# Attention and MLP on one core: Strassen's scheme in the second product of one more pair, and new orders

## The chip, the cores and the metric

The kernel runs on one core of a Trainium2 chip. Five engines work side by side, each through its own queue of instructions: TensorE (PE, with its weight loads shown apart as PEld), VectorE (DVE), ScalarE (ACT), GpSimd (POOL) and SyncE (SP, which issues the DMAs). The metric is device time of one execution in microseconds. The kernel before takes 564.89 us (median of 3 runs, 564.1 to 565.23).

## The reference

Four sequences of 768 tokens, eight heads of 64. Each query sees its neighbours at a distance under 16 and, in place of all the rest, one summary for every block of 32 keys:

```python
k_sum = k.reshape(B, H, nb, block, D).max(axis=3)        # block = 32, nb = 24
v_sum = v.reshape(B, H, nb, block, D).mean(axis=3)
scores_l = scale * np.matmul(q, k.transpose(0, 1, 3, 2)) # kept where |i - j| < 16, else -1e9
scores_s = scale * np.einsum('bhsd,bhnd->bhsn', q, k_sum) + np.log(block)
a = softmax(np.concatenate([scores_l_m, scores_s], axis=-1))
x = np.matmul(a, np.concatenate([v, v_sum], axis=2))     # -> 3072 tokens x 512
h = x @ w_in                                             # 512 x 2048
g = 0.5 * h * (1.0 + erf(h / sqrt(2)))
out = g @ w_out                                          # 2048 x 512
```

All results are fp32. The two weight matrices come as 64-bit floats.

## The kernel before, in words

The 3072 tokens are twelve chunks of 256. A chunk's attention is two units (four heads each), so there are 24 units; a chunk's MLP is a first product (x by `w_in`, `phase1`) and a second (g by `w_out`, `phase2`). For fp32 accuracy each operand is split into a high and a low f16 part, and each product is three f16 matmuls: high by high, high by low, low by high. ACT makes most high parts (steps that end in `_hi`), DVE all low parts (`_lo`), and POOL some casts of k, q, p and x.

A unit: `scores` (PE, into the PSUM tile `ps_s`), `add_mask`, `maximum`, `exponent` (ACT, eight groups of 128), `recip`, then the normalized p is split into `p_h` and `p_l` and turned by two DMA transposes (`turn`), and `values` (PE, into `ps_v`) makes x. The first six units are of another kind: their scores are fp32 matmuls, with the mask added by PE (`f_mask`), and in units 0 to 3 (`TURNED`) p is not split but turned by fp32 matmuls (`p_turn`, `p_keep`), and the values are fp32 as well. For p there are two ways to split: `split_hi` and `split_lo` in eight groups that also normalize, or `p_norm` for the whole tile and then a cast and one `p_lo`.

Chunks 2p and 2p+1 are pair p. For pairs 2 to 5 the first product uses Strassen's scheme: seven products (`product p j m`) for each quarter j of the hidden columns, instead of eight, with sums of x (`sx_add`) and of `w_in` (`t_add`); `keep` copies partial sums out of PSUM, `h_add` adds them. For the last pair, 5, the second product uses the scheme too: sums of g (`s_add`, `s_hi`, `s_lo`), sums of `w_out` (`u_add`, `u_hi`, `u_lo`), and seven products `s_product m j` of 12 matmuls, each 256 columns wide; `phase2` matmuls are 512 wide. PSUM has `ps_s`, `ps_v` and a ring of five banks, handed out in the order in which they come free.

While no data is there yet, PE runs `warm` matmuls on a tile of ones, called fillers here: 54 of them before.

What sets the order on every engine is a list written out by hand (`ORDER`): 1585 steps, each the name of a function and its numbers. The program calls them in that order, every engine takes its instructions in the order of the list, and waits are set by what each instruction reads and writes. Loads and stores go through SP's queue in the list's order too.

Of the kernel before, what the change touches and what calls it, by code (L numbers as in the profile page):

```python
# [88 lines left out]
maximum_p 4, exponent_p 4, recip 3, wi_lo 4 0, p_norm 3, wo_bits 4 0, wi_lo 6 1, p_turn 3 1, f_mask 5,
phase1h 0 2 1, take_hi 2, p_keep 3 1, wi_hi 3 0, p_turn 3 0, wo_bits 4 1, wi_lo 3 1, wi_lo 3 0, wo_bits 4 2,  # L90
recip 4, take_lo 2, wi_bits 0 1, wo_hi 4, p_keep 3 0, gelu 0 1, fetch_w_out 0, load_v 3, fetch_w_in 5, load_v 4,
scores 5, load_vs 3, wo_lo 4, phase1h 0 6 1, values 3, phase1h 0 3 0, phase1h 0 3 1, take_hi 3, wi_bits 0 2,
wo_bits 0 0, take_lo 3, g_hi 0 1, gelu 0 7, wo_bits 0 1, wi_bits 5 0, wi_lo 4 1, wi_hi 0 1, wi_lo 0 1, wo_bits 0 2,
# [15 lines left out]
phase2 0 3, phase2 0 7, phase2 0 6, k_sums 1 0, g_hi 1 2, scores 6, values 5, s_k_hi 8, take_hi 5, store 0 0,
add_mask 6, prep_k_end 1 1, g_lo 1 6, g_lo 1 2, maximum 6, exponent 6, s_q_hi 8, store 0 1, s_k_hi 7, take_lo 5,  # L110
prep_v 1 0, q_lo 7, load_q 9, fetch_v 2 0, k_lo 8, k_sums 1 1, recip 6, prep_v 1 1, q_lo 8, load_vs 6, phase2 1 5,
k_lo 7, phase2 1 3, phase1 2 7, phase2 1 2, phase1 2 2, scores 7, phase1 2 3, g_hi 1 7, split_hi 6, split_lo 6,
g_lo 1 7, add_mask 7, phase2 1 7, scores 8, load_q 10, load_k 9, turn 6 0, q_hi 9, v_hi 6, gelu 2 7, g_hi 2 7,
s_k_hi 9, gelu 2 2, gelu 2 3, v_lo 6, q_lo 9, turn 6 1, phase1 2 4, phase1 2 6, values 6, maximum 7, k_lo 9,
add_mask 8, maximum 8, prep_v 2 0, g_lo 2 7, exponent 7, recip 7, p_norm 7, p_hi 7, load_v 7, load_q 11, put 0 0,
put 0 1, fetch_kx 3 0, exponent 8, recip 8, prep_kx 3 0, load_vs 7, fetch_k 2 0, load_k 10, scores 9, k_hi 10,
take_hi 6, v_hi 7, g_hi 2 2, phase1 2 0, store 1 1, gelu 2 6, s_q_hi 10, g_hi 2 3, g_hi 2 6, gelu 2 0, p_lo 7,
t_add 3 0, take_lo 6, turn 7 0, phase2 1 6, phase1 2 5, v_lo 7, prep_k 2 0, k_lo 10, turn 7 1, load_v 8, values 7,
phase1 2 1, t_add 2 1, split_hi 8, split_lo 8, g_hi 2 0, take_hi 7, take_lo 7, g_lo 2 6, t_add 0 1, gelu 2 5,
g_hi 2 5, g_lo 2 5, add_mask 9, load_k 12, load_k 11, k_hi 11, fetch_k 2 1, gelu 2 4, store 1 0, load_vs 8, put 1 0,  # L120
gelu 2 1, g_lo 2 0, v_hi 8, phase1 3 4, phase1 3 1, q_lo 10, g_lo 2 3, prep_k_end 2 0, maximum 9, fetch_v 3 0,
load_q 12, v_lo 8, k_lo 11, load_v 9, turn 8 0, scores 10, g_lo 2 2, g_hi 2 1, g_lo 2 1, t_add 0 2, add_mask 10,
load_k 13, prep_k 2 1, maximum 10, gelu 3 1, exponent 9, recip 9, phase1 3 3, gelu 3 4, gelu 3 3, g_hi 3 4,
g_hi 3 3, g_lo 3 4, p_norm 9, g_hi 3 1, q_hi 12, k_hi 12, k_lo 12, turn 8 1, fetch_kx 3 1, load_k 14, load_vs 9,
fetch_v 3 1, phase1 3 7, phase1 3 0, phase1 3 6, g_hi 2 4, gelu 3 0, g_hi 3 0, prep_v 3 0, g_lo 3 1, exponent 10,
g_lo 2 4, t_add 0 3, q_hi 11, q_lo 11, g_lo 3 0, phase2 2 0, values 8, phase1 3 2, phase1 3 5, gelu 3 2, k_sums 2 0,
p_hi 9, recip 10, scores 11, p_lo 9, q_lo 12, p_norm 10, turn 9 0, turn 9 1, add_mask 11, prep_kx 3 1, v_hi 9,
gelu 3 6, gelu 3 5, gelu 3 7, g_hi 3 6, g_hi 3 5, s_p_hi 10, x_take 8, sx_hi 2 0, g_lo 3 5, maximum 11, v_lo 9,
# [1147 lines left out]
```

## Time and profile before

| | |
|---|---|
| median of 3 runs | 564.89 us |
| profiled execution | 564.51 us |
| its span, first to last instruction | 562.7 us |
| PE busy | 556.1 us (99%), 6126 matmuls |
| DVE busy | 454.2 us (81%) |
| ACT busy | 379.5 us (67%) |
| POOL busy | 42.2 us (8%) |

The span is the profiled execution without what lies around it, 1.8 us. A busy time is the time in which at least one instruction of the engine was under way. The ends of matmuls are modelled, so how fast PE really goes is read from the steps between starts. In the profile's lists "idle before" is how long the engine had nothing under way before a group's instructions, and what ended that. The columns "out<-in" are the program's tiles; several functions share a line where a helper records them.

### The profile page before, as it was taken

How to read it: one execution, taken by the hardware profiler on the slowest of the kernel's cores; microseconds unless marked ns; L12 is line 12 of the kernel's file. 1: busy time of each engine (PE TensorE's matmuls, PEld its weight loads, DVE VectorE, ACT ScalarE, POOL GpSimd, SP SyncE). 2: the span in 40 equal slices, each digit the busy share in tenths (PEclk: the TensorE clock that was granted, in tenths of full speed). 3: DMA queues.
4: the chain of work that ended last, by engine and by line, in shares of the span. 5: the costliest groups of instructions: out<-in, count | busy, mean ns of one | idle time of the engine just before them, and what ended most of it. 6: DMA issues, size and time to landing. Idle time of an engine off the chain costs nothing.

```text
span 562.7 us, 14579 instructions
## 1 busy us (share of the span) xinstructions
PE 556.1 (99%) x6126; PEld 392.5 (70%) x6126; DVE 454.2 (81%) x699; ACT 379.5 (67%) x940; POOL 42.2 (8%) x50
## 2 busy tenths in 40 slices
PE   9999999999999999999999999999999999999997
PEld 4788886457888555587665767756578756668886
DVE  4999999989999888989989386969745685797750
ACT  2995976548979858879596589795577545346530
POOL 0010000000121001001213000111000010000000
PEclk9999999999999999999999999999999999999999
DMA  8894686677887765434543534512314100001002
GB/s 330 327 406 162 214 245 176 200 226 209 223 255 172 162 163 129 131 64 128 142 131 90 157 80 101 133 32 64 71 54 130 25 2 1 19 1 57 1 1 76
DMA packets 70994, 74.40 MB, mean 132 GB/s; under 512 B 44816, under 2 KB 49808, under 8 KB 70928
## 3 DMA queue, kind: packets, MB, share of 16 engines
q1 hardware_dynamic: 70928, 73.46, 45.9%
q8 instruction: 48, 0.79, 0.6%
q14 instruction: 18, 0.15, 0.1%
HBM read 54.90 MB, written 6.29 MB: 109 GB/s over the span
## 4 chain that ended last, share of the span: by engine, by line
PE 89%; ACT 4%; DMA 3%; DVE 3%; SPq 1%; issue 1%; POOL 0%; ACTq 0%; DVEq 0%; POOLq 0%
PE bank L969 25%; PE bank L1024 10%; PE bank L1026 10%; PE bank L1025 10%; PE bank L1129 5%; PE bank L928 4%; PE bank L941 4%; PE bank L930 4%; PE bank L929 4%; PE ps_v L875 3%; PE bank L917 2%; PE ps_v L1129 2%; PE ps_s L760 2%; PE ps_s L742 2%; ACT s L788 1%; DMA v<-in_vw_dram 1%
## 5 line engine op out<-in xcount | busy, mean ns | idle before, releaser
L1024 PE MATMUL bank<-w_out_h,gh 128*128 128x512 f16 x320 | 121.4, 379 | 0.0
L1025 PE MATMUL bank<-w_out_l,gh 128*128 128x512 f16 x320 | 121.3, 379 | 0.0
L1026 PE MATMUL bank<-w_out_h,gl 128*128 128x512 f16 x320 | 121.3, 379 | 0.0
L1011 DVE SCALAR_TENSOR_TENSOR gl<-g,gh 128x512 f16<-128x512 f32 x92 | 62.1, 693 | 17.8 <-ACT gh L1007 17.7
L969 PEld LDWEIGHTS <-w 128*128 128x128 f16 x640 | 62.0, 98 | 10.5 <-issue 1.5
L969 PEld LDWEIGHTS <-w_in 128*128 128x128 f16 x576 | 55.5, 98 | 11.3 <-issue 0.8
L788 ACT ACTIVATE s<-s,s_top 128x128 f32<-128x128 f32 x144 | 55.6, 389 | 7.7 <-DVE s_top L779 7.6
L1026 PEld LDWEIGHTS <-gl 128*128 128x128 f16 x320 | 31.3, 98 | 37.8
L981 DVE TENSOR_TENSOR g<-bank,late 128x512 f32<-128x512 f32 x48 | 32.9, 685 | 27.9 <-PE bank L969 19.4
L1007 ACT ACTIVATE gh<-g 128x512 f16<-128x512 f32 x92 | 54.8, 623 | 0.5
L1024 PEld LDWEIGHTS <-gh 128*128 128x128 f16 x320 | 31.3, 98 | 33.1
L1025 PEld LDWEIGHTS <-gh 128*128 128x128 f16 x320 | 31.3, 98 | 32.6
L975 ACT ACTIVATE late<-bank 128x512 f32<-128x512 f32 x48 | 28.3, 591 | 32.4 <-PE bank L969 27.5
L969 PE MATMUL bank<-x,w_in 128*128 128x256 f16 x384 | 47.1, 273 | 0.0
L1000 ACT ACTIVATE g<-g 128x512 f32<-128x512 f32 x48 | 29.6, 623 | 21.9 <-DVE g L981 21.9
L969 PE MATMUL bank<-stage,w 128*128 128x256 f16 x320 | 44.1, 273 | 0.0
L969 PE MATMUL bank<-x,w 128*128 128x256 f16 x320 | 43.8, 273 | 0.0
L928 PE MATMUL bank<-x,w_in 128*128 128x256 f16 x144 | 39.3, 273 | 0.0
L929 PE MATMUL bank<-x,w_in 128*128 128x256 f16 x144 | 39.3, 273 | 0.0
L930 PE MATMUL bank<-x,w_in 128*128 128x256 f16 x144 | 39.3, 273 | 0.0
L1000 ACT ACTIVATE g<-bank 128x512 f32<-128x512 f32 x48 | 28.0, 590 | 13.3 <-PE bank L930 7.3
L850 DVE SCALAR_TENSOR_TENSOR v_hl<-v,v_hl 128x1024 f16<-128x1024 f32 x20 | 25.0, 1248 | 6.0 <-ACT v_hl L847 6.0
(206 smaller groups left out, 1146.0 us busy)
## 6 DMA issues: line engine op xcount, KB each, us to landing
v<-in_vw_dram SPq DMA_DIRECT2D x22, 512.0 KB
stage<-in_w_out_dram SPq DMA_DIRECT2D x8, 1024.0 KB
q<-in_qd_dram SPq DMA_DIRECT2D x24, 256.0 KB
out_dram<-ot SPq DMA_DIRECT2D x23, 256.0 KB
k<-in_kd_dram SPq DMA_DIRECT2D x18, 320.0 KB
stage<-in_vb_dram SPq DMA_DIRECT2D x6, 768.0 KB
stage<-in_kp_dram SPq DMA_DIRECT2D x4, 768.0 KB
gh<-in_w_in_dram SPq DMA_DIRECT2D x2, 1024.0 KB
```

The source lines that it names most:

```text
L788: nc.scalar.activation(self.s32[:, gs], score[:, gs], AF.Exp, bias=self.top[:, g : g + 1], scale=QKSCALE, accum_out=self.den[:, g : g + 1],)
L928: nc.tensor.matmul(dst, wh, xh, start=(k == 0), stop=False)
L929: nc.tensor.matmul(dst, wh, xl, start=False, stop=False)
L930: nc.tensor.matmul(dst, wl, xh, start=False, stop=(k == NCC - 1))
L969: nc.tensor.matmul(dst, l, r[:, k], start=(first and e == 0 and k == 0 and n == 0), stop=(k == KH - 1 and n == 2), skip_group_check=True,)
L1000: nc.scalar.activation(g, h, AF.Gelu, scale=1.0 / (SC_X * SC_WI))
L1007: nc.scalar.activation(gh, g_slot(c, i), AF.Copy, scale=SC_G)
L1011: nc.vector.scalar_tensor_tensor(out=gl, in0=g_slot(c, i), scalar=SC_G, in1=gh, op0=ALU.mult, op1=ALU.subtract)
L1024: nc.tensor.matmul(t, gh[:, f, js], w_out_h[:, f, :], start=(n == 0), stop=False)
L1025: nc.tensor.matmul(t, gh[:, f, js], w_out_l[:, f, :], start=False, stop=False)
L1026: nc.tensor.matmul(t, gl[:, f, js], w_out_h[:, f, :], start=False, stop=(n == NFC - 1))
L1129: nc.tensor.matmul(acc[:, t * NH : (t + 1) * NH], a[:, f, js], b[:, f], start=(first and j == 0 and t == 0 and f == 0 and n == 0), stop=(f ...
```

## The change

The order of nearly all steps is new, and with it several functions:

- Pair 4's second product goes by Strassen's scheme as pair 5's does. `s_add`, `s_hi`, `s_lo`, `s_product`, `s_keep`, `s_sum`, `s_end` get the pair as their first number. The sums of `w_out` are made once, earlier, and used by both pairs; they and the sums of g move to other tiles (`homes`, `left`), for which small tiles are joined (`misc`, `kk`). Sixteen `phase2` steps go (80 to 64), 24 `s_product` and two `s_last` come.
- No p is split in eight groups any more: all 21 units that split p use a whole cast on ACT (`s_p_hi`) and a whole `p_lo`. p is normalized by ACT in eight groups for 13 units (`s_norm`, 2 before) and by DVE for 11.
- POOL casts nothing: k, q, p and x are cast on ACT. (POOL also makes no copies of the means of v.)
- The factor 1/8 on the scores moves into `add_mask`, so `maximum` and `exponent` of masked tiles need none; units 0 to 5 keep it.
- Unit 1's scores go to two banks of the ring in place of `ps_s` (`BANKED`). Three units are turned by PE in place of four (`TURNED`). 25 fillers instead of 54. The exponential's table is asked for in `setup`.

```diff
 PAIRS = (2, 3, 4, 5)
+BANKED = (1,)
 WIDE = 6
-TURNED = 4
+TURNED = 3
...
-load_q 0, fetch_k 0 0, load_eye, load_m16, fetch_w_in 2, fetch_k 0 1, fetch_wh 7 1, load_q 1, load_ind,
+fetch_k 0 0, load_m16, load_q 0, fetch_k 0 1, fetch_wh 1 1, load_q 1, fetch_w_in 4, warm 2 9, warm 3 3, f_mask 0,
...
     def setup():
         nc.gpsimd.memset(ones, 1.0)
+        nc.scalar.activation(stats[1][2][:, :1], ones[:, :1], AF.Exp)
...
+        def ps(self, e):
+            if self.banked:
+                return bank.use(f"sc{self.nm}{e}", 4)
+            return ps_s[:, e * QCOLS : (e + 1) * QCOLS]
...
-                out=self.s32.rearrange("p (h j) -> p h j", **shape), in0=m, scalar=SC_WI,
-                in1=ps_s.rearrange("p (h j) -> p h j", **shape), op0=ALU.mult, op1=ALU.add,
+                out=self.s32.rearrange("p (h j) -> p h j", **shape), in0=ps_s.rearrange("p (h j) -> p h j", **shape), scalar=QKSCALE,
+                in1=m, op0=ALU.mult, op1=ALU.add,
...
+            if raw:
+                nc.vector.tensor_scalar_mul(self.top, self.top, QKSCALE)
...
+    SP2 = LAST - 1
 
     def g_slot(c, i):
-        if c // 2 == LAST:
+        if c // 2 >= SP2:
             n = ((9, 7), (5, 8))[c % 2][i // 4]
...
     def g_part(c, i):
-        return (a[:, 2 * i : 2 * i + 2, :].rearrange("p f j -> p (f j)") for a in g_hl[c % 2])
+        if c // 2 == LAST:
+            w = {(0, 0): (0, 0), (0, 1): (1, 1), (1, 1): (1, 0)}[c % 2, i // 4]
+            cs = slice(i % 4 * CH, (i % 4 + 1) * CH)
+            return (a[w][:, :, cs] for a in (w_in_h, w_in_l))
+        return (a[:, 2 * i : 2 * i + 2, :] for a in g_hl[c % 2])
...
+    left = parts_of(flat16)
+    U1, U2, U4, U3 = range(4)
+    homes = {
+        U1: parts_of([misc, late[:, 3072:]]),
+        U2: parts_of([kk, k32[:, 1024:].bitcast(F16)]),
+        U4: left[24:],
+        U3: [a[:, 2 * q : 2 * q + 2, NH:] for q in range(4) for a in (w_out_h, w_out_l)],
+    }
...
+    def s_acc(p, a):
+        if a == SZ:
+            return ps_v if p == LAST else ps_s[:, :QCOLS]
+        return bank.use(f"s{p}{a}", {SX: 19, SY: 5}[a])
...
+    s_sums = {SP2: [a[:, :512] for a in dens], LAST: hsum}
...
-    def s_product(m, j):
-        acc = S_PROD[m][0]()
+    def s_product(p, m, j):
+        acc = s_acc(p, S_PROD[m][0])
         for t in range(CH // P):
-            s_tile(m, j, t, acc)
+            s_tile(p, m, j, t, acc)
```

How the order moves, at three places. On PE at the program's start, from unit 0's scores to its first turn (L742 and L775 are `scores`, L917 and L965 fillers, L828 and L876 `p_turn`, L571 and L596 the sums of v). Before:

```order
L742 MATMUL ps_s<-w_out_l,q_0_83 64x32 x4
L917 LDWEIGHTS ones
L917 MATMUL bank_66<-ones 64x512
...
L742 MATMUL ps_s<-w_out_l,q_1_84 64x32 x4
...
L917 MATMUL bank_63<-ones 64x512
L828 MATMUL bank_64<-mask_sb,s_0_90 128x128 x4
L571 MATMUL bank_65<-w_out_h 88x256 x6
```

and after:

```order
L775 MATMUL ps_s<-w_out_l,q_0_83 64x32 x4
L965 LDWEIGHTS ones
L965 MATMUL bank_65<-ones 64x512
...
L775 MATMUL bank_67<-w_out_l,q_1_84 64x32 x2
...
L965 MATMUL bank_63<-ones 64x512
...
L775 MATMUL ps_s<-misc,q_0_83 64x24 x4
L775 MATMUL ps_s<-w_out_l,q_0_83 64x32 x4
L876 MATMUL bank_64<-misc,s_0_90 128x128 x4
L876 MATMUL bank_65<-misc,s_0_90 128x128 x4
L596 MATMUL bank_63<-w_out_h 88x256 x6
```

Unit 1's scores go to the banks 66 and 67, and the scores of unit 2 (q_0 again) now stand ahead of unit 0's first turn. After unit 0's scores came 30 fillers and now come 12; after unit 1's came 6 and now comes 1.

On ACT at the same place (L788 and L833 are `exponent`, L394 and L416 `wi_hi`, L822 and L870 `s_norm`, L831 and L879 `p_keep`). Before:

```order
L788 ACT_TABLE_LOAD
L788 ACTIVATE s_0_90,s_den_96<-ps_s,s_top_95 128x128 x8
L394 ACTIVATE w_in_71<-w_2_77 128x2x256
L822 ACTIVATE s_0_90<-s_0_90,s_rec_97 128x128 x8
...
L788 ACTIVATE s_1_91,s_den_99<-ps_s,s_top_98 128x128 x8
L394 ACTIVATE late<-w_2_77 128x2x256
L831 ACTIVATE pt<-bank_64 128x512
```

and after:

```order
L382 ACT_TABLE_LOAD
L382 ACTIVATE s_rec_100<-ones 128x1
L833 ACTIVATE s_0_90,s_den_96<-ps_s,s_top_95 128x128 x8
L416 ACTIVATE w_in_72<-w_1_76 128x2x256
L870 ACTIVATE s_0_90<-s_0_90,s_rec_97 128x128 x8
L833 ACTIVATE s_1_91,s_den_99<-bank_66,s_top_98 128x128 x4
L833 ACTIVATE s_1_91,s_den_99<-bank_67,s_top_98 128x128 x4
L416 ACTIVATE w_in_73<-w_0_75 128x2x256
L833 ACTIVATE s_0_90,s_den_96<-ps_s,s_top_95 128x128 x8
L416 ACTIVATE late<-w_0_75 128x2x256
L879 ACTIVATE pt<-bank_65 128x512
```

The table is loaded first, unit 1's exponentials read two banks, and unit 2's come before unit 0's turned p is copied.

On PE in pair 4 (L969 and L1017 are `product`, L1024 to L1026 `phase2`, L1194 `s_product`; gh and gl are the parts of g). Before:

```order
L969 MATMUL bank_66<-stage,w_in_73 128x256
L1024 LDWEIGHTS gh_106
L1024 MATMUL bank_64<-w_out_h,gh_106 128x512
...
L1025 MATMUL bank_66<-w_out_l,gh_106 128x512
L1026 LDWEIGHTS gl_107
L1026 MATMUL bank_66<-w_out_h,gl_107 128x512
```

and after:

```order
L1017 MATMUL bank_65<-stage,w_in_73 128x256
L1194 LDWEIGHTS gh_106
L1194 MATMUL bank_67<-w_out_h,gh_106 128x256
L1194 LDWEIGHTS gh_106
L1194 MATMUL bank_67<-w_out_l,gh_106 128x256
L1194 LDWEIGHTS gl_107
L1194 MATMUL bank_67<-w_out_h,gl_107 128x256
```

Where matmuls of 512 columns stood among pair 5's first products, matmuls of half that width stand now, and the bank they write stays theirs through the pair.

## Rows read from the trace of the kernel before

**Rows 1.** The page's table of engines: busy us, share of the span, instructions.

```profile
PE 556.1 (99%) x6126; PEld 392.5 (70%) x6126; DVE 454.2 (81%) x699; ACT 379.5 (67%) x940; POOL 42.2 (8%) x50
```

**Rows 2.** The page's chain that ended last, shares of the span by engine.

```profile
PE 89%; ACT 4%; DMA 3%; DVE 3%; SPq 1%; issue 1%; POOL 0%; ACTq 0%; DVEq 0%; POOLq 0%
```

**Rows 3.** Stages: length, then busy us (instructions) by engine, clock, DMA share.

```profile
10.00:35.00 25.00, 25.00 (x442) 18.01 (x440) 24.09 (x41) 21.93 (x78) 0.78 (x1) 1.00 0.95 361
60.00:100.00 40.00, 40.00 (x361) 31.20 (x360) 39.62 (x54) 31.13 (x60) 0.00 (x0) 1.00 0.67 196
...
150.00:200.00 50.00, 50.00 (x614) 35.80 (x612) 47.38 (x70) 40.90 (x101) 7.24 (x7) 1.00 0.85 198
200.00:250.00 50.00, 48.01 (x559) 30.57 (x557) 45.74 (x74) 38.95 (x115) 3.09 (x3) 1.00 0.44 112
250.00:300.00 50.00, 50.00 (x600) 34.47 (x598) 45.01 (x64) 42.37 (x95) 10.16 (x9) 1.00 0.50 133
300.00:350.00 50.00, 50.00 (x521) 34.70 (x520) 34.52 (x61) 35.60 (x90) 4.31 (x4) 1.00 0.45 113
...
500.00:562.70 62.70, 59.24 (x512) 49.89 (x510) 35.63 (x56) 25.82 (x48) 0.00 (x0) 0.99 0.09 30
```

Engines there stand in the order PE, PEld, DVE, ACT, POOL.

**Rows 4.** PE in order of time, 126 to 132: start, duration, instruction.

```profile
125.83 0.27 PE L928 MATMUL bank<-x,w_in 128*128 128x256 f16 x1
...
127.80 0.38 PE L1024 MATMUL bank<-w_out_h,gh 128*128 128x512 f16 x1
...
130.39 0.27 PE L928 MATMUL bank<-x,w_in 128*128 128x256 f16 x1
```

**Rows 5.** The chain in order of time: start, length, piece and its instructions.

```profile
9.46 6.16 PE bank L917 x28
...
529.11 5.24 PE bank L1129 x48
...
556.62 2.63 PE bank L1129 x24
```

**Rows 6.** Groups on PE: count | busy us, mean ns | idle before.

```profile
L875 PE MATMUL ps_v<-pt,v_hl 128*64 128x64 f16 x960 | 19.1, 197 | 0.0
...
L1129 PEld LDWEIGHTS <-gh 128*128 128x128 f16 x128 | 12.5, 98 | 1.4
...
L828 PE MATMUL bank<-mask_sb,s 128*128 128x128 f32 x64 | 8.5, 278 | 0.0
...
L875 PE MATMUL ps_v<-pt,v_hl 128*64 128x64 f32 x64 | 2.6, 226 | 0.2 <-issue 0.2
```

**Rows 7.** Groups on DVE and ACT, in the same columns.

```profile
L1011 DVE SCALAR_TENSOR_TENSOR gl<-g,gh 128x512 f16<-128x512 f32 x92 | 62.1, 693 | 17.8 <-ACT gh L1007 17.7
...
L805 ACT ACTIVATE p_h<-s,s_rec 128x128 f16<-128x128 f32 x88 | 26.8, 390 | 0.0
...
L810 DVE SCALAR_TENSOR_TENSOR p_l<-s,s_rec,p_h 128x128 f16<-128x128 f32 x88 | 24.4, 348 | 0.0
...
L840 DVE TENSOR_TENSOR p_l<-s,p_h 128x1024 f16<-128x1024 f32 x9 | 10.9, 1216 | 1.2 <-POOL p_h L834 1.2
...
L718 ACT ACTIVATE qh<-q 128x512 f16<-128x512 f32 x11 | 6.8, 619 | 5.0 <-DMA q<-in_qd_dram 5.0
...
L822 ACT ACTIVATE s<-s,s_rec 128x128 f32<-128x128 f32 x16 | 4.9, 392 | 0.1
...
L837 ACT ACTIVATE p_h<-s 128x1024 f16<-128x1024 f32 x2 | 2.1, 1047 | 0.0
```

**Rows 8.** In order of time, from the start and from 57 on.

```profile
5.92 1.75 DVE L530 TENSOR_REDUCE ks<-w_out_l 128x48 f32<-128x1536 f32 x1 [5.92 <-DMA w_out_l<-in_kp_first_dram]
...
9.53 1.22 DVE L776 TENSOR_REDUCE s_top<-ps_s 128x8 f32<-128x1024 f32 x1 [1.85 <-PE ps_s L742]
...
11.04 1.28 ACT L788 ACT_TABLE_LOAD   x1 [11.04 <-DVE s_top L779]
...
59.93 0.27 PE L928 MATMUL bank<-x,w_in 128*128 128x256 f16 x1
```

More of the change, by code (lines that the diff above doesn't have):

```diff
@@ L89 @@
[L89 to L93, printed above, removed]
@@ L109 @@
[L109 to L113, printed above, removed]
@@ L114 @@
[L114 to L128, printed above, removed]
@@ new lines @@
+s_k_hi 15, keep 2 0 2, store 3 1, load_vs 13, put 3 1, exponent 14, h_add 2 0 3, product 2 0 4, product 2 0 3,
+gelu 5 0, g_hi 5 0, s_k_hi 16, v_hi 13, t_lo 1 1, k_lo 15, q_lo 16, values 12, recip 14, p_lo 13, q_lo 15,
+prep_kx 3 4, phase2 3 6, product 2 1 5, product 2 2 1, scores 15, h_add 2 0 1, v_lo 13, g_lo 5 0, k_lo 16, gelu 4 0,
+g_hi 4 0, g_lo 4 0, add_mask 15, store 3 0, keep 2 1 1, gelu 4 4, keep 2 2 0, gelu 5 4, t_hi 2 1, g_hi 4 4,
+product 2 1 7, keep 2 1 2, t_hi 2 0, x_take 12, product 2 3 1, scores 16, product 2 1 4, turn 13 1, turn 13 0,
@@ new lines @@
+g_lo 7 0, load_v 19, load_vs 19, gelu 6 5, gelu 7 5, v_hi 19, keep 3 2 1, v_lo 19, keep 3 3 0, store 5 1, x_take 18,
+product 3 2 7, product 3 2 5, g_hi 7 5, g_hi 7 1, turn 19 0, load_v 20, turn 19 1, put 5 0, load_q 23, keep 3 2 2,
+g_lo 7 5, h_add 3 2 3, add_mask 21, k_lo 22, put 5 1, load_vs 20, s_norm 20, g_hi 6 5, s_q_hi 22, sx_hi 4 1,
+product 3 3 6, product 3 2 3, product 3 2 4, values 19, h_add 3 2 1, q_lo 22, scores 22, g_lo 7 1, sx_hi 4 0,
+keep 3 3 1, product 3 3 7, gelu 6 6, gelu 6 2, g_hi 6 6, gelu 7 6, phase2 6 0, g_lo 6 5, sx_lo 4 0, u_add 0 0,
@@ new lines @@
+phase2 6 3, scores 23, phase2 6 2, v_hi 21, sx_hi 4 5, g_hi 6 7, keep 4 0 0, sx_hi 4 4, sx_lo 4 4, u_add 0 3,
+v_lo 21, s_norm 21, s_p_hi 21, gelu 7 3, g_lo 6 7, p_lo 21, u_add 0 4, maximum 22, sx_lo 4 5, add_mask 23,
+sx_add 4 6, product 4 0 6, keep 4 0 1, exponent 22, product 4 0 2, phase2 6 7, phase2 6 6, values 20, u_hi 0 0,
+store 6 0, g_hi 7 3, load_v 22, load_vs 22, v_hi 22, store 6 1, g_hi 7 6, h_add 4 0 0, recip 22, sx_lo 4 3,
+p_norm 22, maximum 23, sx_hi 4 6, sx_lo 4 6, g_lo 7 3, x_take 20, v_lo 22, product 4 1 1, product 4 0 7, turn 21 0,
@@ L793, in exponent_p @@
         def exponent_p(self):
-            self.exponent(ps_s)
+            if not self.banked:
+                return self.exponent(ps_s)
+            for e in range(2):
+                self.exponent(self.ps(e), e)
         def recip(self):
```

469 lines of the change are left out of this document (255 added, 214 removed).

## Prediction

> **What bounds the kernel now.** I read the page's table of engines first, then the chain of waits, then the busy time by stage, and last the groups of instructions by line. TensorE (PE) is busy for 556.1 us of a span of 562.7 [rows 1], and the chain that ends last is 89% PE [rows 2]. A busy PE is not a full PE, so I looked at steps from start to start: eighteen 256-column matmuls take from 125.83 to 127.80, 109.4 ns each, and twelve 512-column ones from 127.80 to 130.39, 215.8 ns each [rows 4]. Per column that is 0.427 and 0.421 ns, at a granted clock of 1.00 [rows 3], the 2.4 GHz level. There is no slack inside a busy PE there, so what shortens its work shortens the kernel as long as the others keep up. PE's idle time is 2.0 us in 200:250 and 3.5 us behind its last matmul [rows 3]; the last piece begins at 556.62 [rows 5], and behind it stand only a copy and a store.
>
> The others do not keep up everywhere. VectorE (DVE) is busy for 24.1 of 25 us in 10:35, 39.6 of 40 in 60:100 and 47.4 of 50 in 150:200 [rows 3]. In the first 100 us it is a second bound, and PE fills its gaps there with 54 fillers. ScalarE (ACT) is densest in 250:300, 42.4 of 50, where GpSimd (POOL) works 10.2 us beside it.
>
> **The change part by part.** The sum is made against the profiled execution, 564.5 us: a span of 562.7 and 1.8 around it.
>
> Second product of the last-but-one pair. 192 matmuls of 512 columns go (16 `phase2` steps of 12) and 336 of 256 columns come. By the step above 192 x 0.2158 = 41.4 us go; for the half-wide ones the last pair's own rows count, 48 in 5.24 us [rows 5], so 336 x 0.1092 = 36.7 us come. Term: -4.7 us, all of it on PE's path, where nothing hides it. Its price on the others, 16 additions and 12 more low parts at 0.69 us on DVE and 12 more high parts at 0.62 on ACT [rows 7], lies after 400, where both have room (ACT 25.8 of 62.7 us from 500 on, [rows 3]). The narrow place there is the ring of five banks, of which the pair's sums hold two while the next pair begins.
>
> A rule speaks against this edit. By rows, 256 and 512 columns cost the same per column [rows 4], and the weight load of a half-wide matmul, 98 ns [rows 6], still fits under its 109 ns. The Trainium skill (TensorE: Matmul & The Clock Gate, section Back-to-back issue gap) gives a sustained spacing of about 81 ns at 128 columns and 131 at 512, set by load and matmul together, which would make wide matmuls far cheaper per column. By an estimate from that page, with 98 ns at 256 columns, this term would be 32.9 - 25.2 = +7.7 us. The trace disagrees at 512 columns, 215.8 ns against 131, and the measurement decides.
>
> Unit 3. PE no longer turns its p in fp32; it is split, and turned by DMA, like the later units'. PE loses a quarter of the turns of four units (8.5 us) and a quarter of their fp32 values (2.6 us in the row shown; I take the same for the other half, which is as many), and gets 48 of the small f16 matmuls, 48/960 of 19.1 us [rows 6]: -2.1 - 1.3 + 1.0 = -2.4 us of PE work. DVE gets a whole low part of p (1.22, [rows 7]) and one of v, and `values 3` gets a new wait, for two DMA transposes that stand in SyncE's queue behind loads of 0.25 to 1 MB. Behind it on PE wait a `phase1h`, the scores of unit 5 and all of chunk 1.
>
> Fillers and the new start. 29 of 54 fillers go; 28 took 6.16 us [rows 5], so 6.4 us of PE. But a filler stands where PE would wait, so this and unit 3's 2.4 are worth only what the start itself gains. The place to read it is the first `phase1` of chunk 1, at 59.93 [rows 8]: from there on PE has the same work before and after, but for the second product. That step follows `take_lo 3` on DVE, and DVE after 9.53 [rows 8] hardly waits. The DVE instructions up to and including it sum to 53.3 us before (64 steps) and 50.7 after (61), by the mean durations of their groups. That is 2.6 us sooner. DVE's first work waits until 5.92 for K [rows 8], which stands behind a 256 KB load of q and now goes first; with that and a shorter gap before 9.53 I take 0.7 more. The table load at 11.04, 1.28 us [rows 8], moves into set-up, and unit 1's scores get banks of their own instead of waiting for unit 0's exponentials to leave `ps_s`; both relieve ACT and PE, and give nothing while DVE is the later one. Term for unit 3 and the start together: -3.3 us. Bounds: -8.8 (6.4 + 2.4) if PE never misses the fillers, and +2.5 (a loss) if DVE's two new parts for unit 3 push everything behind them. I take -3.3, since DVE's 99% in 60:100 leaves no more.
>
> Whole p splits, no casts on POOL, the scale of scores. For eleven units eight-part splits go. On ACT, eight rows of 0.39 become eight equal ones that normalize (L805 and L822, [rows 7]), and 19 whole copies of 1.05 come on top: +20 us. The 31 casts of k, q and x from POOL cost ACT 0.62 to 0.72 each: +20. With the pair's high parts (+7.5) and four copies of v and its means (+4), ACT gets +51 us: 379.5 becomes 431, 78% of the new span. DVE loses 24.4 us of L810, gets 12 whole low parts (14.6) and the pair's 28 rows (19.3), and drops 18 multiplications of 0.17, since the scale moves into the mask's addition: about +10, to 464 us, 84%. While both stay ahead of PE this costs nothing on its path. The cover is thin in one place: between `product 3 1 4` and `phase2 6 4` the new order holds 37.6 us of ACT by these rows against 26.9 of PE, so ACT must enter that stretch ahead. Bounds: -2.0, if the waits in 200:250 go and none come, and +21, if ACT is never ahead (third rival). I take 0: the row nearest is today's, 2.0 us of waits inside, and I let as much come as goes.
>
> Sum: -4.7 - 3.3 + 0 = -8.0, so 556.5 for a profiled execution. The median of the runs, 564.89, lies 0.4 above the profiled one; I predict 557.0.
>
> **The rivals.**
> All of it comes back, because DVE does not set the start. Then -4.7 - 8.8 - 2.0 = -15.5: 549 to 552. For it: PE is at 40.0 of 40 in 60:100, beside DVE's 39.6, so it need not be waiting for DVE there. Against it: DVE at 99%. Chance 0.18.
>
> The start gives nothing and banks run short. Pair 5's products have three banks in place of five; if in each of four rounds PE waits for a `keep` and an `h_add` (0.6 + 0.7 us, estimated from the 0.62 and 0.69 in [rows 7]), 5.2 us stand against 4.7: 563 to 566. For it: three reuses in the new order with only 0.9 to 1.3 us of PE work between a bank's last write and its next use. Against it: the order before has one such reuse of 1.3 us in pair 2, and PE idles only 2.0 us in that whole stretch. Chance 0.08.
>
> ACT becomes the bound, and the kernel slower. The places are chunk 2's `phase1` (33.7 us of ACT in the new order against 23.4 of PE) and the end of pair 3 (37.6 against 26.9). If ACT cannot work ahead there, because its exponentials wait for scores that PE makes just before, PE waits 10.3 + 10.7 = 21 us: 564.5 - 8.0 + 21 = 577.5; half of it is 567. It decides from 8 us of such waits on. For it: ACT's 42.4 of 50 in 250:300 before POOL's 10.2 come over. Against it: 35.6 of 50 in the next stretch [rows 3] leaves room on both sides. Chance 0.12.
>
> Half-wide matmuls cost more than half. If their 98 ns of weight load lay bare, 336 x 98 ns = 32.9 us come on top: 589. The last pair's 336 of this shape show nothing of it [rows 5]. The skill's rule would show in this way. Chance 0.01.
>
> That the change does not do what it says is out: the new order has 768 matmuls of 512 columns in place of 960, and 25 fillers.
>
> **How the numbers follow.** The forecast, with 553 to 561 as its own range, has 0.61. What a measurement of this kernel can tell from no change is about 0.2%, 1.1 us. Faster: 0.61 + 0.18 + half of the bank rival, 0.04, and 0.02 for a mild ACT rival, 0.85. Within 0.2%: the other half, 0.04. Slower: 0.10 + 0.01 = 0.11. The range for 8 in 10 reaches into the first rival below and through most of the second above: 550.5 to 563.5.
>
> **What would show it.** Right: 256 matmuls in each of the three 512-column lines and 672 half-wide ones at 109 ns; the first `phase1` of chunk 1 at 56 to 57; PE idle for under 4 us between there and its last matmul; DVE above 97% in 10:60. The start's term is wrong if chunk 1 begins at 59 or later, or before 55. The third part is wrong if waits of PE for ACT's `keep`, `gelu` or `store` sum to over 4 us. The prediction as a whole falls if PE idles more than 8 us after 60.

## The result, and the profile after

The changed kernel takes 556.77 us (median of 4 runs, 556.61 to 557.98) beside 564.5 for the kernel before on the same chip: ratio 0.987, 95% interval 0.9847 to 0.9892. Predicted were 557.0. The profiled execution took 556.6 with a span of 554.8, 7.9 us less than before. The total came out as forecast, but two of the three terms behind it did not: their errors cancel.

The page's table of engines and the chain that ended last, for [rows 1, 2]:

```profile
PE 544.9 (98%) x6241; PEld 402.8 (73%) x6241; DVE 453.2 (82%) x638; ACT 425.3 (77%) x1005; POOL 0.8 (0%) x9
...
PE 94%; DMA 3%; DVE 1%; issue 1%; ACT 0%; SPq 0%; ACTq 0%; DVEq 0%
```

Stages, in the columns of [rows 3]:

```profile
10.00:35.00 25.00, 20.41 (x407) 15.90 (x405) 22.33 (x39) 20.11 (x84) 0.00 (x0) 0.93 0.97 372
35.00:60.00 25.00, 24.96 (x473) 21.05 (x471) 24.07 (x37) 23.21 (x56) 0.00 (x0) 1.00 0.79 263
150.00:200.00 50.00, 50.00 (x608) 35.36 (x606) 46.92 (x61) 47.68 (x120) 0.00 (x0) 1.00 0.78 203
200.00:250.00 50.00, 50.00 (x627) 33.03 (x626) 43.99 (x61) 46.32 (x115) 0.00 (x0) 1.00 0.59 143
300.00:350.00 50.00, 50.00 (x608) 35.36 (x606) 30.31 (x46) 47.32 (x124) 0.00 (x0) 1.00 0.42 95
350.00:400.00 50.00, 49.55 (x545) 33.38 (x544) 40.51 (x60) 44.80 (x111) 0.00 (x0) 1.00 0.37 90
500.00:554.80 54.80, 51.11 (x469) 45.58 (x466) 19.90 (x31) 14.15 (x27) 0.00 (x0) 1.00 0.11 35
```

Two things stand out. In 10:35 PE, busy for all 25.0 us before, now idles for 4.6, and its clock is 0.93. And in 200:250, where it idled for 2.0, it idles no more, although ACT is busier than anywhere before.

The new matmuls, from the chain in order of time, and groups that answer to [rows 5 to 7]:

```profile
515.74 5.24 PE bank L1194 x48
...
531.46 2.62 PE bank L1194 x24
```

```profile
L1080 PE MATMUL bank<-w_out_h,gh 128*128 128x512 f16 x256 | 97.1, 379 | 0.0
...
L888 DVE TENSOR_TENSOR p_l<-s,p_h 128x1024 f16<-128x1024 f32 x21 | 25.5, 1212 | 1.7 <-ACT p_h L885 1.7
...
L885 ACT ACTIVATE p_h<-s 128x1024 f16<-128x1024 f32 x21 | 22.1, 1052 | 1.0 <-DVE gl L1067 0.8
...
L965 PE MATMUL bank<-ones 128*64 128x512 f16 x25 | 8.2, 489 | 0.9 <-POOL ones L381 0.9
```

48 half-wide matmuls still take 5.24 us, 109.2 ns each, and each 512-column line has 256 left. All 21 splits of p are whole, at the durations of [rows 7].

The start, for [rows 8]: PE in order of time.

```profile
13.10 0.26 PE L775 MATMUL bank<-misc,q 64*64 64x24 f32 x6
14.29 0.18 PE L775 MATMUL bank<-misc,q 64*64 64x24 f32 x1 [0.94 <-issue]
...
16.38 0.34 PE L775 MATMUL ps_s<-w_out_l,q 64*64 64x64 f32 x8 [0.76 <-DMA q<-in_qd_dram]
...
20.34 0.60 PE L876 MATMUL bank<-misc,s 128*128 128x128 f32 x3 [0.72 <-issue]
...
23.37 1.05 PE L876 MATMUL bank<-misc,s 128*128 128x128 f32 x8
...
28.89 1.67 PE L876 MATMUL bank<-misc,s 128*128 128x128 f32 x8 [2.18 <-issue]
30.49 1.98 PE L923 MATMUL ps_v<-pt,v 128*64 128x64 f32 x32
...
39.40 1.15 PE L923 MATMUL ps_v<-pt,v_hl 128*64 128x64 f32 x32
...
58.25 0.28 PE L976 MATMUL bank<-x,w_in 128*128 128x256 f16 x1
```

Three waits are put down to "issue": the profile shows nothing that PE waits for. Two lie inside a step, between matmuls that read the same tiles. After the longest the same work is slower: half of a turn takes 1.67 us at 28.89 and 1.05 at 23.37, a `values` 1.98 and later 1.15. That is the lower level of the clock: it is granted at 0.50 in 29.5:32.5.

VectorE's `take_lo 3`, whose result chunk 1 reads, before and after:

```profile
58.46 0.68 DVE L887 SCALAR_TENSOR_TENSOR x<-ps_v,x 128x512 f16<-128x512 f32 x1
```

```profile
56.04 0.69 DVE L935 SCALAR_TENSOR_TENSOR x<-ps_v,x 128x512 f16<-128x512 f32 x1
```

It comes 2.4 us sooner. Chunk 1's first `phase1` comes only 1.7 sooner (58.25 beside 59.93), 1.5 us after this step has ended; before it was 0.8. And VectorE itself was held up on the way, by unit 0's x, whose `values` (30.49 above) PE finished late:

```profile
32.51 0.60 ACT L932 ACTIVATE x<-ps_v 128x512 f16<-128x512 f32 x1 [3.34 <-PE ps_v L923]
33.14 0.69 DVE L935 SCALAR_TENSOR_TENSOR x<-ps_v,x 128x512 f16<-128x512 f32 x1 [1.99 <-ACT x L932]
```

Counting every instruction of TensorE in the trace from the first, the three waits stand behind numbers 449, 705 and 961, 256 apart. (The expectation of `sums_early` calls this a count of matmuls and weight loads together; by the third wait it has seven semaphore and drain instructions in it as well.) The trace also has packets of 16,384 bytes in a queue of kind "instruction". The place between two blocks of 256 is called an edge from here on. When a packet started, and the last start of PE ahead of its edge and the first behind it, in us:

| number | before: packet, PE | after: packet, PE | `sums_late_edge_2` (below) |
|---|---|---|---|
| 449 | 12.35, 17.52 to 17.52 | 12.00, 13.14 to 14.29 | 11.44, 13.24 to 13.76 |
| 705 | 20.86, 25.62 to 25.63 | 17.89, 19.35 to 20.34 | 17.45, 17.99 to 19.68 |
| 961 | 27.25, 32.99 to 33.00 | 26.26, 26.49 to 28.89 | 23.58, 27.44 to 27.66 |
| 1217 | 35.66, 37.74 to 38.18 | 31.57, 38.60 to 38.60 | 29.52, 34.96 to 34.97 |

Wherever PE waits here, it goes on 2.2 to 2.6 us after the packet's start. Theory FETCH: PE gets its instructions in blocks of 256, and where many small matmuls run beside full DMA queues the next block is late. Before, 54 fillers (108 instructions, 13.6 us) kept PE behind the packets. Rivals: these are waits for data, or only VectorE's slack seen from PE.

### The profile page after: what moved, and what is told of

Read it like the earlier page. It is cut to its first block, busy times and chain, and to the rows that moved or that the text cites. A ratio compares the mean times of both kernels' runs of the same rounds, so it can differ in the third digit from the quotient of the medians.

```text
span 554.8 us, 14751 instructions
## 1 busy us (share of the span) xinstructions
PE 544.9 (98%) x6241; PEld 402.8 (73%) x6241; DVE 453.2 (82%) x638; ACT 425.3 (77%) x1005; POOL 0.8 (0%) x9
## 4 chain that ended last, share of the span: by engine, by line
PE 94%; DMA 3%; DVE 1%; issue 1%; ACT 0%; SPq 0%; ACTq 0%; DVEq 0%
PE bank L1017 25%; PE bank L1080 10%; PE bank L1081 10%; PE bank L1082 10%; PE bank L1194 9%; PE ps_v L923 4%; PE bank L976 4%; PE bank L989 4%; PE bank L978 4%; PE bank L977 4%; PE ps_s L793 3%; PE ps_s L1194 2%; PE ps_v L1194 2%; PE ps_s L775 1%; DMA q<-in_qd_dram 1%; PE bank L876 1%
## 5 line engine op out<-in xcount | busy, mean ns | idle before, releaser
L1080 PE MATMUL bank<-w_out_h,gh 128*128 128x512 f16 x256 | 97.1, 379 | 0.0
L1081 PE MATMUL bank<-w_out_l,gh 128*128 128x512 f16 x256 | 97.0, 379 | 0.0
L1082 PE MATMUL bank<-w_out_h,gl 128*128 128x512 f16 x256 | 97.0, 379 | 0.0
L1017 PEld LDWEIGHTS <-w 128*128 128x128 f16 x640 | 62.0, 98 | 9.3
L1017 PEld LDWEIGHTS <-w_in 128*128 128x128 f16 x576 | 55.9, 98 | 8.6
L833 ACT ACTIVATE s<-s,s_top 128x128 f32<-128x128 f32 x144 | 55.8, 394 | 0.1
L1067 DVE SCALAR_TENSOR_TENSOR gl<-g,gh 128x512 f16<-128x512 f32 x76 | 51.0, 683 | 4.0 <-ACT gh L1063 3.9
L1063 ACT ACTIVATE gh<-g 128x512 f16<-128x512 f32 x76 | 46.6, 626 | 3.4 <-PE bank L1081 2.8
L1082 PEld LDWEIGHTS <-gl 128*128 128x128 f16 x256 | 25.1, 98 | 30.2
L1017 PE MATMUL bank<-x,w_in 128*128 128x256 f16 x384 | 46.6, 273 | 0.0
L1080 PEld LDWEIGHTS <-gh 128*128 128x128 f16 x256 | 25.0, 98 | 26.7
L1081 PEld LDWEIGHTS <-gh 128*128 128x128 f16 x256 | 25.1, 98 | 26.0
L1017 PE MATMUL bank<-stage,w 128*128 128x256 f16 x320 | 44.0, 273 | 0.0
L1017 PE MATMUL bank<-x,w 128*128 128x256 f16 x320 | 43.6, 273 | 0.0
L870 ACT ACTIVATE s<-s,s_rec 128x128 f32<-128x128 f32 x104 | 31.8, 391 | 0.4 <-DVE s_rec L848 0.4
```

The costliest lines, as they stand in the source:

```text
L833: nc.scalar.activation(self.s32[:, gs], score[:, ss], AF.Exp, bias=self.top[:, g : g + 1], scale=scale, accum_out=self.den[:, g : g + 1],)
L1017: nc.tensor.matmul(dst, l, r[:, k], start=(first and e == 0 and k == 0 and n == 0), stop=(k == KH - 1 and n == 2), skip_group_check=True,)
L1063: nc.scalar.activation(gh, two(g_slot(c, i)), AF.Copy, scale=SC_G)
L1067: nc.vector.scalar_tensor_tensor(out=gl, in0=two(g_slot(c, i)), scalar=SC_G, in1=gh, op0=ALU.mult, op1=ALU.subtract)
L1080: nc.tensor.matmul(t, gh[:, f, js], w_out_h[:, f, :], start=(n == 0), stop=False)
L1081: nc.tensor.matmul(t, gh[:, f, js], w_out_l[:, f, :], start=False, stop=False)
```

## The experiments

**The block by itself** (`tiny_matmuls`):

```diff
+load_q 0, load_q 1, tiny 0 1024, load_q 0, flood 16, tiny 1 1024, finish
```

> Not the kernel's work: 1024 matmuls of 64x32 in fp32 with a weight load each while no other DMA runs, then the same 1024 while sixteen loads of 1 MB are under way; a 128-row store of zeros but for one tile stands for the output. Theory FETCH: in both halves a wait at every 256th instruction of TensorE; without other transfers a block of 256 takes 2 to 3 us in all, with them 4 to 9 us, and the instruction packets of 16,384 bytes in the trace are as many as the blocks. Rival: TensorE goes at an even pace in both halves, and what the changed kernel waited for was data.

PE in the half without other DMA, and in the half with it:

```profile
3.54 26.67 PE L1065 MATMUL ps_s<-q 64*64 64x32 f32 x991 [3.54 <-DMA q<-in_qd_dram]
...
69.85 3.64 PE L1065 MATMUL ps_s<-q 64*64 64x32 f32 x128 [2.84 <-issue]
76.32 3.63 PE L1065 MATMUL ps_s<-q 64*64 64x32 f32 x128 [2.83 <-issue]
```

Under load every 128 pairs end in a wait of 2.6 to 2.8 us, at all seven edges from number 4545 to 6081; a block takes 6.2 to 6.5 us. Without load the blocks run on almost without a gap (0 to 0.7 us), in 3.4 to 4.0. A packet takes 0.9 to 1.4 us in both halves. What differs is when it starts: 0.4 to 1.7 us after PE began the block ahead of it without load, 3.6 to 4.1 us after under load. The rival, an even pace in both halves, is out. The idle half came out slower per block than expected, since these matmuls take 26 ns each by themselves.

**Fillers where PE waits** (`bridge`):

```diff
+warm 5 4, p_turn 0 0, ...
+warm 4 10, f_mask 3, scores 3, p_turn 1 0, ...
```

> The changed kernel with 14 fillers more: 4 ahead of unit 0's turn, 10 (2.2 us) ahead of unit 3's mask and scores. Theory FETCH: the waits stand at the same counts of TensorE's instructions (705 and 961), now within other steps (the second within unit 3's scores, not ahead of unit 1's turn); the fillers' 3.0 us take their place, so that chunk 1 starts no later than at 58.3, and if the clock stays at 1.00 in 10:35, some 1.5 us sooner, 56.5 to 57.5: total 555 to 556.5. Rival WAIT: the 2.4 us at 26.5 are a wait of unit 1's turn for another engine's result (VectorE's maximum of unit 3 ends at 28.8): then the wait stays ahead of that turn and ends at 28.8 to 28.9, and the count of instructions there is 981 or so. Rival FILLERS COST: TensorE's time sets the start, 14 more fillers are 3.0 us more: chunk 1 at 61, total 559.8.

556.38 us (4 runs, 555.08 to 557.3; ratio 0.9852, 0.9831 to 0.9874). The wait ahead of unit 1's turn is gone, of the one at edge 705 only 0.25 us are left, and the clock holds:

```profile
10.00:35.00 25.00, 23.32 (x432) 17.36 (x430) 22.54 (x39) 21.11 (x89) 0.00 (x0) 1.00 1.00 381
```

So 3.0 us of fillers cost nothing, and neither rival holds. But chunk 1 began at 58.55, not at 56.5 to 57.5: at the edge 1985, now inside unit 5's scores, PE waited 1.5 us at 56.7. Filling one edge had moved another into small matmuls.

**All 29 fillers back** (`fillers_back`):

```diff
+warm 4 6, f_mask 0, ...
-warm 0 12, ... warm 1 1
+warm 0 30, ... warm 1 6
```

> The changed kernel with 29 fillers put back, 54 in all as before: 6 more ahead of unit 0's mask, 18 more after unit 0's scores, 5 more after unit 1's. The prediction held that a filler costs TensorE nothing where it would wait anyway, and worth only what the start gains by others. Theory FETCH: they take the place of the waits for instruction blocks (3.4 us before 30 in the changed kernel go below 0.8) and hold the granted clock at 1.00, but the first 24 also put off the scores of units 0 and 1: chunk 1 at 58.5 to 60.5, total 557 to 559. Rival FILLERS COST: all 29 come on top, 6.3 us: chunk 1 at 64.5, total 563. Rival DVE: VectorE's list sets the start, chunk 1 as before within 0.5 us, total 556.8.

561.04 us (6 runs, 559.0 to 562.28; ratio 0.9937, 0.9918 to 0.9955), more than FETCH gave. Chunk 1 began at 59.21 as it said, and the edges up to 1217 cost nothing (those at 1473 and 1985 cost 1.0 and 0.9). But in the profiled run PE then stopped at number 3265 (193 + 12 x 256), 67 us later:

```profile
125.21 0.22 PE L793 MATMUL ps_s<-kk,qh 64*64 64x128 f16 x3
128.53 0.26 PE L793 MATMUL ps_s<-kk,qh 64*64 64x128 f16 x1 [3.10 <-issue]
128.73 0.61 PE L1080 MATMUL bank<-w_out_h,gh 128*128 128x512 f16 x1
129.13 0.63 PE L1081 MATMUL bank<-w_out_l,gh 128*128 128x512 f16 x1
```

and for seven matmuls the step was 0.36 to 0.43 us in place of 0.216. 58 instructions more had shifted every later edge; this one fell into a unit's scores. The 29 fillers cost 4.3 us by the medians, neither 6.3 nor nothing. In the profiled run 1.0 us of the loss is the later chunk 1; the rest arose behind that, where this is the only long wait.

**VectorE against TensorE** (`unit3_by_matmul`):

```diff
-TURNED = 3
+TURNED = 4
-s_p_hi 3, ... turn 3 0, ... v_hi 3, ... p_lo 3, turn 3 1, ... v_lo 3
+take_hi 2, p_turn 3 0, p_turn 3 1, p_keep 3 0, p_keep 3 1
```

> The changed kernel with unit 3's p turned by TensorE in fp32 again (no split of its p and v, no DMA transposes): TensorE gets 2.4 us more work, VectorE 2.4 us less (a low part of p and one of v, 1.22 each). Theory PE: from 30 us on TensorE sets when chunk 1 begins, its idle time in 35:60 is near nothing, so chunk 1 starts 1.5 to 2.5 us later, total 558.3 to 559.3. Rival DVE: VectorE sets it by its last low part of x (ended 0.6 us before chunk 1's x is used), so chunk 1 starts 1 to 2.4 us sooner, total 554.5 to 556.

559.1 us (4 runs; ratio 0.9902, 0.9886 to 0.9919): slower, as theory PE said. In 35:65 VectorE now waits for PE's values:

```profile
DVE x L935 <- ACT x L932: 5.9, 1, 5.9
ACT x L932 <- PE ps_v L923: 3.1, 1, 3.1
```

In the profiled run, the slowest of the four (561.47, the others 558.88 to 559.19), chunk 1 began at 62.82, later than work alone explains: a wait of 1.4 us at 48.5 and the half-speed clock of 10:35 (0.86) add to it. By the medians, splitting unit 3's p was worth about 2.3 us.

**Unit 1's banks** (`no_banks_unit1`; unit 1's probabilities then come from unit 2's scores, which take `ps_s` first):

```diff
-BANKED = (1,)
+BANKED = ()
```

> The changed kernel with unit 1's scores in ps_s again, in place of two banks of the ring. TensorE then waits with unit 1's mask until unit 0's exponentials have left ps_s, at 13.1 in place of 10.5. The prediction gave this part nothing while VectorE is the later one. Theory HIDDEN: 2.4 us of waiting there take the place of the waits at the edges of instruction blocks (1.1 and 0.9 us); chunk 1 at most 1 us later, total 556.8 to 557.8. Rival: the whole delay of 2.6 us goes through to unit 1's and 2's exponentials and chunk 1: 559 to 560.

562.39 us (6 runs; ratio 0.9949, 0.9929 to 0.9968), above both. PE's two longest waits in 5:60:

```profile
PE ps_s L730 <- ACT s L833: 2.7, 1, 2.7
PE bank L876 <- DVE s L865: 2.6, 1, 2.6
```

The first is the delay that was put in; the second, of unit 1's turn for its normalized p, follows from it. The granted clock in 10:35 is 0.76, and chunk 1 began at 63.49. The banks, which the prediction gave nothing, are worth up to 5.6 us in this order.

**The casts** (`pool_casts`):

```diff
-s_k_hi 6, ... s_q_hi 9, ... sx_hi 2 4, ...
+k_hi 6, ... q_hi 9, ... p_sx_hi 2 4, ...
```

> The changed kernel with the 31 casts of k, q and x on GpSimd again that stood there before (9 of k, 7 of q, 15 of x); the order of the steps stays. Theory COLLISION: the 2.0 us of inner waits of the kernel before came from these casts, which are slow themselves and lengthen VectorE's instructions beside them: TensorE's inner waits after 60 us grow from 0.45 to 1.5 to 3 us, VectorE's busy time grows by 4 to 9 us, total 557.8 to 560. Rival ORDER: the new order alone removed the waits; inner waits stay under 0.8 us and the total is 556.5 to 557.3.

556.91 us (4 runs; ratio 0.9864, 0.9844 to 0.9883): no difference. Busy time from 60 to 554, with the casts on POOL and in the changed kernel:

```profile
60.00:554.00 494.00, 491.92 (x5254) 362.25 (x5253) 410.90 (x564) 364.36 (x837) 29.12 (x31) 1.00 0.43 114
```

```profile
60.00:554.00 494.00, 490.67 (x5244) 361.26 (x5241) 403.78 (x562) 380.53 (x866) 0.00 (x0) 1.00 0.43 113
```

VectorE does get slower beside POOL, by 6.2 us over the whole run (459.4 beside 453.2; in this window 7.1, with two instructions more), but PE does not wait for it: from chunk 1's first `phase1` to the last matmul it takes 492.40 us, beside 492.59. COLLISION falls for the waits, ORDER holds. (The Trainium skill, SBUF — State Buffer, section SBUF: two separate sides, says that a VectorE instruction with two SBUF inputs and one of GpSimd that reads SBUF lock each other out, and that the one that starts first holds the lock to its end. The trace agrees: of q's 18 low parts two took 1160 and 983 ns, and these are the two that began while a cast of POOL was under way; the median is 684, and without POOL none took over 693.)

**The pair's matmuls** (`more_strassen_work`):

```diff
             s_tile(p, m, j, t, acc)
+            if p == SP2 and m == 6:
+                s_tile(p, m, j, t, acc)
```

> The changed kernel with one of the new products of pair 4's second product done twice: 4 of its steps get 12 matmuls of 256 columns more, 48 in all, 5.24 us by the step of 109.2 ns. (The output of pair 4 then holds that product twice.) Theory PE: from 60 us on TensorE's work is the time, so that the term of -4.7 us is worth what its matmuls take: total 5.0 to 5.4 us above the changed kernel, 561.8 to 562.2. Rival SLACK: VectorE (47.8 of 50 us in 400:450) or ScalarE sets the pace there and TensorE's saved work was partly a wait: total under 560.

562.34 us (4 runs; ratio 0.9951, 0.9933 to 0.9969), just above the range of theory PE. From chunk 1's first `phase1` to the last matmul the trace has 499.12 us beside 492.59: 6.5 more, of which 1.3 are two waits that were shorter in the changed kernel, at 58.4 (an edge) and at 354 (for a transpose of p). The rest, 5.2, is the 5.24 put in. TensorE is the pace there; SLACK is out.

**Real work in the gaps.** First `sums_early`, then `sums_early_2`:

```diff
-p_turn 0 0, p_turn 0 1, sum_vt 0
+sum_vt 0, p_turn 0 0, p_turn 0 1
-p_turn 1 0, ... sum_vt 1
+sum_vt 1, p_turn 1 1, f_mask 3, scores 3, p_turn 1 0
```

> The changed kernel with two steps moved: the sums of v (sum_vt 0 ahead of unit 0's turn, sum_vt 1 ahead of unit 1's first turn), 2.75 us of matmuls each in few instructions, to stand where TensorE waited in the changed kernel (0.9 us at 19.4, 2.4 us at 26.5). Theory FETCH: TensorE's instructions come in blocks of 256 by a DMA packet of 16,384 bytes, asked for when the block before is begun, and late while the DMA engines are 99% busy; TensorE waits for them in the changed kernel at its instructions number 449, 705 and 961 (of matmuls and weight loads together, 256 apart), 4.5 us in all, and the granted clock falls after the last. Then work ahead of the edge of a block hides the wait: the waits at 705 and 961 together under 1 us, granted clock 1.00 in 10:35, first phase1 of chunk 1 at 54.5 to 56.5 (58.25 in the changed kernel), total 553 to 555. Rival DVE: the start is set by VectorE's list, and TensorE's waits there only show its slack; then chunk 1 still starts at 57.5 or later and the total is 556.3 to 557.

558.41 us (5 runs; ratio 0.9886, 0.9867 to 0.9905). Above both theories, with chunk 1 at 60.30. The edges 705 and 961 cost nothing, but a new wait came, for a table loaded late, and the clock fell with it (0.86 in 10:35):

```profile
20.18 5.39 PE L596 MATMUL bank<-w_out_h 128*88 128x256 f32 x12 [2.35 <-DMA w_out_h<-in_mask_dram]
```

```diff
+load_ind, fetch_wh 6 1
-sum_vt 1, p_turn 1 1, f_mask 3
+p_turn 1 1, sum_vt 1, f_mask 3
```

> The sums of v moved again, with what the first try lacked: their table of blocks (load_ind) is loaded ahead of the weights, sum_vt 0 stands ahead of unit 0's turn, sum_vt 1 between unit 1's first turn and unit 3's mask. Theory FETCH: the wait for the table (2.4 us at 17.6 in the first try) goes, the edges at 705 and 961 fall into work whose blocks are there, granted clock 1.00 in 10:35, chunk 1 at 55.5 to 57, total 554 to 555.5. Rival: another wait takes their place again (VectorE's in-order list is put off by unit 3's later scores), chunk 1 at 58 or later, total 556.5 to 558.5.

557.2 us (4 runs; ratio 0.9874, 0.9855 to 0.9893): the rival. The edges stayed free of waits, but q then came late (2.0 us at 14.7, clock 0.86 in 10:35), and unit 3's later scores made unit 4's mask wait 1.5 us at 35.6 for unit 3's exponentials.

**Scores of unit 5 moved** (`bridge_2`, and in `sums_late_edge`):

```diff
-scores 5, ... phase1 1 1
+phase1 1 1, scores 5
```

> The bridge of 14 fillers again, and unit 5's scores moved behind the first phase1 of chunk 1, so that 2.6 us of long matmuls stand where the edge of a block (number 1985) cost 1.5 us in the bridge. Theory FETCH: that wait goes, nothing takes its place; the fourth phase1 step's end comes 1 to 1.5 us sooner than in the bridge; total 554.6 to 556. Rival: the waits of the bridge were data, and TensorE waits for x or the scores elsewhere; total 556 to 557.

> No fillers more, but real work in the gaps: unit 2's q is loaded ahead of a weight of 512 KB; sum_vt 1 and unit 1's first turn stand behind unit 3's scores, so that the edge 961 falls inside the sum; unit 3's exponentials stand ahead of unit 0's take on ScalarE; unit 5's scores stand behind the first phase1 of chunk 1. Theory FETCH: 1.7 us of the sum cover the wait at 961, which falls to 0.5 to 1.5 us, the granted clock stays at 1.00 in 10:35, and 2 us of dense work behind 30 us are gone: total 553 to 555. Rival: unit 3's chain (maximum, exponentials, mask of unit 4) or VectorE's list then sets the start: total 556 to 557.5.

560.2 us (6 runs; ratio 0.9913, 0.9892 to 0.9935) and 560.29 (6 runs; 0.9911, 0.9897 to 0.9926): both missed, by one mistake of mine. A low part of `w_out` goes into the tile that holds k, so the moved scores wait for it, and then read that part in place of k:

```profile
54.38 0.27 PE L976 MATMUL bank<-x,w_in 128*128 128x256 f16 x1
...
61.13 0.49 PE L775 MATMUL ps_s<-w_out_l,q 64*64 64x64 f32 x8 [3.20 <-DVE w_out_l L420]
```

The first row, of `sums_late_edge`, was worth the run: with the 1.5 us of scores ahead of it chunk 1 would begin at 55.9.

**The same without the mistake** (`sums_late_edge_2`):

```diff
-... fetch_wh 6 1, load_eye, load_q 2
+... load_q 2, fetch_wh 6 1, load_eye
-p_turn 1 1, f_mask 3, scores 3, p_turn 1 0, ... sum_vt 1
+f_mask 3, scores 3, sum_vt 1, p_turn 1 1, p_turn 1 0
-take_hi 0, ... exponent_p 3
+exponent_p 3, take_hi 0
```

> The last try without its misstep: unit 5's scores stand where they stood in the changed kernel (they read k from a tile that a low part of w_out then takes). What stays: unit 2's q loaded ahead of a weight, sum_vt 1 and unit 1's first turn behind unit 3's scores, unit 3's exponentials ahead of unit 0's take. In the last try chunk 1 began at 54.4 without these scores' 1.54 us ahead of it, so 55.9 with them, against 58.25 in the changed kernel. Theory FETCH (the start is worth what the waits for blocks and the clock cost): first phase1 of chunk 1 at 55.7 to 57, granted clock 1.00 in 10:35, total 553.8 to 555.5; a wait at edge 1985, now inside that phase1, of 0.3 to 1.5 us. Rival: VectorE's last low part of x sets the start (it ended at 55.9 in the last try), so that no more than 1 us of it is gained: chunk 1 at 57.2 or later, total 555.8 to 557.

554.29 us (5 runs, 554.15 to 556.1; ratio 0.9833, 0.9816 to 0.985), the fastest: its slowest run, 556.1, is below the changed kernel's fastest, 556.61. Its stages, and PE in order of time:

```profile
10.00:35.00 25.00, 22.58 (x484) 17.61 (x486) 22.28 (x40) 22.62 (x92) 0.00 (x0) 1.00 1.01 384
35.00:60.00 25.00, 24.12 (x430) 20.24 (x424) 24.90 (x38) 22.92 (x50) 0.00 (x0) 1.00 0.83 256
```

```profile
19.68 0.60 PE L876 MATMUL bank<-misc,s 128*128 128x128 f32 x3 [1.42 <-issue]
...
25.86 2.82 PE L596 MATMUL bank<-w_out_h 128*88 128x256 f32 x12
...
39.22 1.26 PE L989 MATMUL bank<-x,w_in 128*128 128x256 f16 x10 [0.59 <-DVE w_in L420]
...
55.94 0.28 PE L976 MATMUL bank<-x,w_in 128*128 128x256 f16 x1
```

The edge 961 lies inside the sum and costs nothing (0.22 us from start to start, as in the rest of it), the clock holds, and chunk 1 begins 2.3 us sooner; against the kernel before, the median gained 2.4 more (10.1 us under it, in place of 7.7). Part of this, 0.8 us, is the wait for q, which is gone; the moves were not tried one by one. Now PE meets VectorE: it waits 0.8 us for low parts at 38 to 41, and VectorE is busy for 24.90 of 25. The next gain has to be looked for there, or at the edge 705, which still costs 1.6.

## Why the prediction came out right, step by step

**What bounds the kernel.** Right from 60 us on: work put into PE comes back one for one (5.2 of 5.24 in the trace, 5.6 by the medians).

**Second product, -4.7.** Right. 192 x 0.2158 and 336 x 0.1092 stand in the trace as priced, and the step of the half-wide matmuls is unchanged. The rule of the Trainium skill weighed there (TensorE: Matmul & The Clock Gate, section Back-to-back issue gap) again finds no support: 215.8 ns at 512 columns here, 131 there.

**Start and unit 3, -3.3.** Wrong in size: -1.7 (59.93 to 58.25). The step that failed is that the start is worth what VectorE's list gains, "while DVE is the later one". VectorE gained 2.4 (I took 2.6 + 0.7; it idles 2.7 us in 10:35 now, 0.9 before), but PE became the later one. VectorE's work up to `take_lo 3` fell by more than I had summed, from 54.7 us (not 53.3) to 50.7 in the traces; 2.0 of these 4.0 us went into its wait for unit 0's x, that is, for PE. From 28.89 until chunk 1 PE does not wait at all. PE's account: 29 fillers -6.5 (start to start, 13.6 to 7.1), unit 3 -2.4 (my estimate; the experiment gave 2.3 by medians); against it edges of blocks +4.0 (4.4 less the 0.4 of before), half-speed clock +1.7 (0.62, 0.83 and 0.25 in the turn, the `values` and the sum behind 28.89), q +0.8, the sums of k +0.3. That makes -2.1, where -1.7 was measured; 0.4 stay unassigned. I had looked for waits of data only. What stands between PE's instructions was in the trace before too, at 37.74, 0.4 us long.

The Trainium skill (Runtime: NRT & Kernel Launch, section Instruction fetch mechanics) states the blocks of 256 instructions and 16 KiB, fetched by the sequencer's own DMA queue, and calls an edge "mostly hidden". The trace agrees on the size; the edges here cost up to 3.1 us, so the measurement decides on the rest.

**Third part, 0.** Wrong by 1.75: from chunk 1's first `phase1` to the last matmul it is 499.04 before and 492.59 after, 6.45 less, of which 4.7 are the product. The waits in 200:250 went, and next to nothing came (0.45 us at 353, for a transpose of p). "As much come as goes" had no row behind it. That the casts left POOL is not the reason (`pool_casts`); with them back, the new order still has no such waits. Which of its moves removes them was not tried. VectorE's 453.2 us in place of 464 come from the casts in good part: with them on POOL it is 459.4. (The terms that I listed there add up to +6.4, which would be 460.6, and not to "about +10".)

-1.7 - 6.45 + 0.2 (a longer tail) = -7.9. The two errors, +1.6 and -1.75, cancel, and so 557.0 stood beside 556.77. The sum was right by chance.

**The rivals.** All of it back: no, but its argument, that PE need not be waiting for VectorE, was the sounder one for the start, and 2.3 us more were to be had. Banks short: PE is busy for 100.0 us in 400:500. ACT as the bound: it came denser than I feared (47.7 of 50 in 150:200), and still PE did not wait; a share of 95% beside a full PE is no bound as long as the order lets it work ahead. Half-wide matmuls dearer: no.

**What was to show it.** First `phase1` at 56 to 57: missed, at 58.25, on the side of "wrong from 59" but short of it. PE's idle time behind it under 4 us: held. VectorE above 97% in 10:60: missed, 46.4 of 50.

## What to carry to other kernels

Fillers, and any long work with few instructions, can hide more than waits for data: before taking them out, count the engine's instructions and see whether small matmuls then outrun the blocks that bring them. Where PE waits for "issue" inside a step, look for the distance of 256, and put long matmuls across that edge; every instruction added ahead shifts all later edges. And when a total fits, check its terms: here two were off by 1.6 us and more.
